# Loading the head's W1 chunks of block 0 in pairs, as 1 KB runs

## The chip, the cores and the metric

One core of one Trainium2 chip runs the whole kernel. The metric is the device time of one execution in microseconds (us). The three sets of experiments ran on chips 5, 14 and 12, so times are compared within a set, and a kernel of one set with one of another only by way of their ratios to the kernel before. A profile shows one execution; its span, from the first instruction to the last, is 1.7 to 1.8 us shorter than that execution's time.

## The reference

```python
y = _layernorm(x)                                             # x: 1 x 2048 x 1024, bf16
h = gelu(einsum("bsd,df->bsf", y, w1) + b1)                   # w1: 1024 x 3584
return einsum("bsf,fd->bsd", h, w2) + b2                      # w2: 3584 x 1024
```

## The kernel before

Both products are done by a Strassen-Winograd scheme: seven half-size products in place of eight, at the price of sums of the inputs (T1 to T4 of the normalized x, S1 to S4 of W1) on the vector engine (DVE). TensorE (PE) is busy nearly all the time. A Python scheduler orders the recorded operations on each engine by their latest useful start, and a packer with a random seed places the buffers.

The argument is about the head, the first 31 us: x is loaded in eight tiles (0 to 7) and normalized; tiles 0 to 3 are transposed on PE, tiles 4 to 7 by DMA (I call these transposes 1 to 4). W1 comes in chunks of 256 columns, each with an upper half of rows (h0) and a lower half (h1), 256 KB each.

```python
def w1_load(b, ch, which, due=None):          # "A1": left columns of W1, "A2": right columns
    i = int(which[1]) - 1
    o = i * FH + ch * 256
    for h in range(2):                        # h0, h1: 4 x 256 columns per partition, runs of 512 B
        bf = W[b, ch, f"{i + 1}{h + 1}"] = M.alloc(KH * 512, f"w1{i}{h}_{b}{ch}")
        pr.due = due if h == 0 else None
        dma("SP", lambda e, h=h, bf=bf: e.dma_start(v3(bf, 0, KH * 512, KH, BF16),
            w1v[:, h * KH:(h + 1) * KH, o:o + 256]), [], [bf.c()], P * KH * 512, None, f"w1{i}{h}_{b}{ch}")
# w1_sums(b, ch): S1 = A21 + A22, S2 = S1 - A11, S3 = A11 - A21, S4 = A12 - S2     (DVE, L799)
# tsum(b, t):     T1 = B12 - B11, T2 = B22 - T1, T3 = B22 - B12, T4 = B21 - T2     (DVE, L763, per tile)
# ... the head, cut:
for ch in range((RH + 1) // 2 - 1):           # chunks 0 to 4: not gated
    w1_load(0, ch, "A1", ...)
# ... waves: first products of rows 0 to 6, one token tile at a time, while the tiles arrive
if t == W_GATE[0]:                            # gated: not before wave 3's first part
    gate[0] = pr.last_pe
    w1_load(0, 5, "A1")                       # chunk 5, h0 and h1
    gate[0] = None
if t == W_GATE[1]: ...                        # the same with w1_load(0, 0, "A2")
# ...
for r in range(RH):                           # RH = 11: 15 products of 4 matmuls
    if r + 1 >= WAVE_ROWS and r + 1 < RH:
        p1(r + 1)                             # first product: needs h0
    p2(r)                                     # second product: needs h1
warm(1, bank=7, full=True)                    # one filler matmul
# then row 0's sixth product, the first that needs T2 (all four tiles) and S2 (chunk 0)
```

## Time and profile before

| | before |
|---|---|
| median of the first three executions | 333.7 us (333.12 to 333.77) |
| the profiled execution | 334.54 us, span 332.8 us |
| PE busy | 326.7 us, 98% of the span |
| first of the 15 products starts (same profile) | 16.06 us |
| long run of PE after the filler starts (same profile) | 30.77 us |

### The profile page before, as it was taken

What the parts mean: (1) busy time and instruction counts of PE and PEld (TensorE: products, weight loads), DVE (VectorE), ACT (ScalarE), POOL (GpSimd) and SP (SyncE); (2) the same over time, 40 slices, a digit from 0 to 9 for tenths busy, and PEclk for the clock granted to TensorE, in tenths of its full rate; (3) what the DMA queues carried; (4) which work ended last, traced back from release to release, by engine and by line L of the source; (5) the groups of instructions that cost most, each with busy time, mean ns of one, the idle gap of its engine ahead of it and who ended that gap; (6) DMA issues with size and microseconds to landing.
All of it is one profiled execution on the core that took longest, in us unless ns stands there. A gap on an engine that the chain in (4) does not pass through costs nothing.

```text
span 332.8 us, 4656 instructions
## 1 busy us (share of the span) xinstructions
PE 326.7 (98%) x1672; PEld 154.8 (47%) x1673; DVE 298.9 (90%) x478; ACT 181.0 (54%) x308; POOL 13.7 (4%) x31
## 2 busy tenths in 40 slices
PE   8998999999999999999999999999999999999996
PEld 5843444444444444444444444444444444444445
DVE  5968999999999975999699998999999959999994
ACT  4795999997677776677776553561211204211411
POOL 2210120111000000000000000000000000000000
PEclk9999999999999999999999999999999999999999
DMA  7997997979999899989969464555699767999867
GB/s 220 326 181 196 282 290 221 295 215 301 307 291 327 281 294 342 310 297 386 336 187 259 147 185 115 163 156 176 176 238 254 221 198 183 273 279 292 192 149 164
DMA packets 121184, 80.73 MB, mean 243 GB/s; under 512 B 35146, under 2 KB 112586, under 8 KB 121162
## 3 DMA queue, kind: packets, MB, share of 16 engines
q1 hardware_dynamic: 118106, 79.32, 84.3%
q10 hardware_dynamic: 3056, 1.11, 1.3%
q8 instruction: 13, 0.21, 0.3%
q14 instruction: 9, 0.07, 0.1%
HBM read 48.70 MB, written 24.38 MB: 220 GB/s over the span
## 4 chain that ended last, share of the span: by engine, by line
PE 90%; DMA 5%; DVE 3%; SPq 1%; issue 0%; POOL 0%
PE ps L934 45%; PE ps L1276 44%; DMA mem<-mem 2%; DMA mem<-in_x_dram 2%; DMA mem<-in_w_dram 1%; DVE st_sb L688 1%; PE ps L1283 1%; DVE mem L763 1%; SPq L787 1%; DVE mem L695 0%; SPq L658 0%; POOL rstd_sb L692 0%; SPq L745 0%; DVE mv_sb L690 0%; PE ps L1156 0%
## 5 line engine op out<-in xcount | busy, mean ns | idle before, releaser
L934 PE MATMUL ps<-mem 128*128 128x512 f16 x756 | 164.1, 379 | 1.4 <-DMA mem<-in_w_dram 1.4
L1276 PE MATMUL ps<-mem 128*128 128x512 f16 x672 | 145.7, 379 | 0.0
L934 PEld LDWEIGHTS ps<-mem 128*128 128x128 f16 (+1 forms) x756 | 73.7, 98 | 90.8 <-ACT mem L843 1.8
L859 ACT COPY mem<-ps 128x512 f32<-128x512 f32 x111 | 64.5, 588 | 76.0 <-PE ps L1276 62.1
L1276 PEld LDWEIGHTS ps<-mem 128*128 128x128 f16 (+1 forms) x672 | 65.8, 98 | 79.3
L843 ACT ACTIVATE mem<-ps,b_sb 128x512 f16<-128x512 f32 x112 | 73.5, 691 | 22.6 <-DVE ps L867 12.9
L867 DVE TENSOR_TENSOR ps<-ps,mem 128x512 f32<-128x512 f32 x84 | 58.0, 695 | 11.7 <-ACT mem L859 8.6
L1091 DVE TENSOR_TENSOR mem<-mem 128x2048 f16<-128x2048 f16 (+1 forms) x56 | 59.3, 1085 | 1.6 <-PE ps L1276 1.6
L799 DVE TENSOR_TENSOR mem<-mem 128x1024 f16<-128x1024 bf16 (+1 forms) x56 | 37.9, 685 | 1.8 <-DMA mem<-in_w_dram 1.2
L1000 DVE TENSOR_TENSOR mem<-mem 128x512 f16<-128x512 f16 (+5 forms) x84 | 37.3, 462 | 0.4
L1103 DVE TENSOR_TENSOR mem<-mem 128x2048 f16<-128x2048 f16 (+1 forms) x32 | 33.6, 1087 | 0.4 <-PE ps L934 0.4
L850 ACT COPY ps<-ps 128x512 f32<-128x512 f32 x31 | 17.7, 570 | 23.4 <-DVE mem L1175 14.8
L1175 DVE TENSOR_TENSOR mem<-ps,mem 128x512 f32<-128x512 f32 x24 | 16.5, 685 | 3.9 <-PE ps L1276 3.7
L688 DVE BATCH_NORM_STATS2 st_sb<-mem 128x6 f32<-128x512 bf16 x24 | 15.4, 674 | 4.0 <-DMA mem<-in_x_dram 4.0
L984 DVE TENSOR_TENSOR mem<-mem 128x2048 f16<-128x2048 bf16 (+1 forms) x16 | 17.3, 1082 | 0.0
L1128 DVE TENSOR_TENSOR mem<-ps,mem 128x512 bf16<-128x512 f32 x22 | 15.0, 688 | 1.3 <-PE ps L1276 1.2
L763 DVE TENSOR_TENSOR mem<-mem 128x512 f16<-128x512 f16 x32 | 12.1, 419 | 2.5 <-DMA mem<-mem 2.3
L692 POOL TENSOR_TENSOR rstd_sb<-mv_sb,nhalf 128x1 f32<-128x1 f32 x12 | 8.4, 699 | 45.6 <-DVE mv_sb L690 44.4
L1262 ACT COPY ps<-b_sb 128x512 f32<-128x512 f32 x6 | 3.5, 588 | 8.2 <-DVE mem L1175 8.0
L695 DVE TENSOR_SCALAR mem<-mem,mv_sb,rstd_sb 128x1024 f16<-128x1024 bf16 (+1 forms) x13 | 6.6, 518 | 1.4 <-POOL rstd_sb L692 1.4
L1351 PE MATMUL ps<-mem 128*128 128x128 f16 x112 | 7.3, 219 | 0.3 <-DMA mem<-in_w_dram 0.3
L1306 PE MATMUL ps<-const-bfloat16-1.0 128*128 128x128 bf16 (+1 forms) x35 | 6.0, 350 | 1.4 <-PEq L1607 0.8
(45 smaller groups left out, 73.3 us busy)
## 6 DMA issues: line engine op xcount, KB each, us to landing
mem<-in_w_dram SPq DMA_DIRECT2D x80, 256.0 KB, 4.9
mem<-w_scr SPq DMA_DIRECT2D x28, 448.0 KB, 3.9
w_scr<-mem SPq DMA_DIRECT2D x21, 512.0 KB, 5.1
w_raw<-mem SPq DMA_DIRECT2D x12, 512.0 KB, 5.6
mem<-w_raw SPq DMA_DIRECT2D x12, 448.0 KB, 4.4
mem<-in_w_dram SPq DMA_DIRECT2D x9, 448.0 KB, 4.1
mem<-in_x_dram SPq DMA_DIRECT2D x15, 256.0 KB, 4.3
out_dram<-mem SPq DMA_DIRECT2D x12, 256.0 KB, 3.9
```

The costliest lines, as they stand in the source:

```text
L688: op("DVE", 0.62, lambda e, i=i, h=h: e.bn_stats(st_sb[:, i, 6 * h:6 * (h + 1)], v16(b, h * D, D, BF16)), r=[b.c(h)], w=[c_st[i][h]], name ...
L799: op("DVE", d_tt(n), lambda e: e.tensor_tensor(out=o[0], in0=a[0], in1=bb[0], op=f), r=[a[1], bb[1]], w=[o[1]], name=f"w1S{k}_{ch}")
L843: op("ACT", A_GELU, lambda e: e.activation(out=dst, in_=banks[bank][:, :], func=ACT.Gelu_apprx_tanh, bias=b1_sb[:, f:f + 1], scale=1.0), r ...
L850: op("ACT", A_CP, lambda e: e.copy(out=banks[dst][:, :], in_=banks[src][:, :]), r=[bank_c[src]], w=[bank_c[dst]], name=name, lat=A_LAT)
L859: op("ACT", A_CP, lambda e: e.copy(out=v16(a, 0, 2048, F32), in_=banks[src][:, :]), r=[bank_c[src]], w=[a.c()], name=name, lat=A_LAT)
L867: op("DVE", D_PS, lambda e: e.tensor_tensor(out=banks[dst][:, :], in0=banks[src][:, :], in1=v16(a, 0, 2048, F32), op=ALU.add), r=[bank_c[s ...
L934: i = e.matmul(banks[bank][:, :], lhsT=lv[:, k, :], rhs=rv[:, k, :], start=(fresh and k == 0), stop=(k == KH - 1), skip_group_check=True)
L984: op("DVE", d_tt(2 * self.n), lambda e: e.tensor_tensor(out=vd, in0=va, in1=vb, op=ALU.subtract), r=self.cells(a) + self.cells(bb), w=self ...
L1000: tt = lambda o, a, c: (lambda e: e.tensor_tensor(out=o, in0=a, in1=c, op=ALU.subtract))
L1091: op("DVE", d_tt((k1 - k0) * 512), lambda e, a=a, bb=bb, o=o: e.tensor_tensor(out=o, in0=a[0], in1=bb[0], op=f), r=a[1] + bb[1], w=[t.c(z) ...
L1103: op("DVE", d_tt((k1 - k0) * 512), lambda e, va=va, vb=vb, vd=vd: e.tensor_tensor(out=vd, in0=va, in1=vb, op=f), r=h_cells(b, a, s, k0, k1 ...
L1276: i = e.matmul(banks[bank][:, :], lhsT=bv[:, k, :], rhs=av3[:, k, :], start=(fresh and k == 0), stop=(k == KQ - 1), skip_group_check=True)
```

## The change

Its intent: fewer, longer loads where the DMA queue of the head is full, and the lower half of chunk 5 earlier. Chunks 0 to 3 keep single h0 loads; h1 of chunks 0 and 1, h1 of 2 and 3, h0 of 4 and 5 and (gated) h1 of 4 and 5 become pairs of 512 KB with 1 KB runs, each in one buffer that lives until both chunks have let it go. The packer's seed changes.

```diff
-SEED = 18
+SEED = 17
+            def w1_block(b, chs, i, h, due=None):
+                n = len(chs)
+                o = i * FH + chs[0] * 256
+                bf = M.alloc(KH * 512 * n, f"w1{i}{h}_{b}{chs[0]}")
+                uses = [n]
+                ...
+                dma("SP", lambda e: e.dma_start(v3(bf, 0, KH * 512 * n, KH, BF16), w1v[:, h * KH:(h + 1) * KH, o:o + 256 * n]),
+                    [], [bf.c()], P * KH * 512 * n, None, f"{'w1' if n == 1 else 'W1'}{i}{h}_{b}{chs[0]}")
 ...
-            for ch in range((RH + 1) // 2 - 1):
-                w1_load(0, ch, "A1", (None, W_DUE[ch]) if ch < len(W_DUE) else None)
+            for ch in range(4):
+                w1_block(0, (ch,), 0, 0, (None, W_DUE[ch]) if ch < len(W_DUE) else None)
+            w1_block(0, (0, 1), 0, 1)
+            w1_block(0, (2, 3), 0, 1)
+            w1_block(0, (4, 5), 0, 0)
 ...
-                    w1_load(0, (RH + 1) // 2 - 1, "A1")
+                    w1_block(0, (4, 5), 0, 1)
```

More of the change, by code (lines that the diff above doesn't have):

```diff
@@ L778, in build, with w1_load, w1_view @@
             W = {}
-            def w1_load(b, ch, which, due=None):
-                i = int(which[1]) - 1
-                o = i * FH + ch * 256
-                for h in range(2):
-                    bf = W[b, ch, f"{i + 1}{h + 1}"] = M.alloc(KH * 512, f"w1{i}{h}_{b}{ch}")
-                    pr.due = due if h == 0 else None
-                    dma("SP", lambda e, h=h, bf=bf: e.dma_start(v3(bf, 0, KH * 512, KH, BF16), w1v[:, h * KH:(h + 1) * KH, o:o + 256]),
-                        [], [bf.c()], P * KH * 512, None, f"w1{i}{h}_{b}{ch}")
-                pr.due = None
+            w1_part = {}
+            def w1_block(b, chs, i, h, due=None):
[3 more added lines that the diff above has]
+                uses = [n]
+                for z, ch in enumerate(chs):
+                    W[b, ch, f"{i + 1}{h + 1}"] = bf
+                    w1_part[b, ch, f"{i + 1}{h + 1}"] = z, n, uses
+                pr.due = due
+                dma("SP", lambda e: e.dma_start(v3(bf, 0, KH * 512 * n, KH, BF16), w1v[:, h * KH:(h + 1) * KH, o:o + 256 * n]),
+                    [], [bf.c()], P * KH * 512 * n, None, f"{'w1' if n == 1 else 'W1'}{i}{h}_{b}{chs[0]}")
+                pr.due = None
+            def w1_load(b, ch, which):
+                for h in range(2):
+                    w1_block(b, (ch,), int(which[1]) - 1, h)
+            def w1_view(b, ch, k, dt):
+                bf = W[b, ch, k]
+                z, n, _ = w1_part.get((b, ch, k), (0, 1, None))
+                return v3(bf, 0, KH * 512 * n, KH, dt)[:, :, z * 256:(z + 1) * 256], bf.c()
             def w1_sums(b, ch):
                 n = KH * 256
-                A = lambda k: (v16(W[b, ch, k], 0, n * 2, BF16), W[b, ch, k].c())
-                S = lambda k: (v16(W[b, ch, k]), W[b, ch, k].c())
+                A = lambda k: w1_view(b, ch, k, BF16)
+                S = lambda k: w1_view(b, ch, k, F16)
                 def mk(k, a, bb, f):
@@ L808, in lhs1 @@
                 k = {1: "11", 2: "12", 4: "22", 3: 4, 5: 1, 6: 2, 7: 3}[q]
-                bf = W[b, ch, k]
-                return v3(bf, 0, KH * 512, KH, BF16 if q in (1, 2, 4) else F16)[:, :, rr:rr + P], bf.c()
+                v, c = w1_view(b, ch, k, BF16 if q in (1, 2, 4) else F16)
+                return v[:, :, rr:rr + P], c
             def w1_drop(b, ch, which):
-                M.free(W.pop((b, ch, which)))
+                bf = W.pop((b, ch, which))
+                uses = w1_part.pop((b, ch, which), (0, 1, [1]))[2]
+                uses[0] -= 1
+                if not uses[0]:
+                    M.free(bf)
             H = {}
@@ L1325, in build @@
             dma("SP", lambda e: e.dma_start(b1r_sb[FT:NBR, :], b2.rearrange("(t p) -> t p", p=P)), [], [c_b2r], D * 2, None, "b2")
-            for ch in range((RH + 1) // 2 - 1):
-                w1_load(0, ch, "A1", (None, W_DUE[ch]) if ch < len(W_DUE) else None)
+            assert (RH + 1) // 2 == 6
+            for ch in range(4):
[3 more added lines that the diff above has]
+            w1_block(0, (4, 5), 0, 0)
             for i in range(4):
```

## The prediction

> **What bounds the kernel now.** I began with the page's busy shares, because they say how much there is to win at all:
>
> ```profile
> PE 326.7 (98%) x1672; PEld 154.8 (47%) x1673; DVE 298.9 (90%) x478; ACT 181.0 (54%) x308; POOL 13.7 (4%) x31
> ```
>
> TensorE (PE) is busy nearly the whole span: only 332.8 - 326.7 = 6.1 us are not matmul time. PE's waits show which part of that waits for something:
>
> ```profile
> PE ps L934 <- DMA mem<-in_w_dram: 1.4, 1, 1.4
> PE ps L1306 <- PEq L1607: 0.8, 1, 0.8
> PE ps L1306 <- DVE st_sb L688: 0.6, 1, 0.6
> PE ps L1351 <- DMA mem<-in_w_dram: 0.3, 1, 0.3
> ```
>
> The middle two belong to the start. The 1.4 and the 0.3 us are waits for W1 loads, which the change touches. The chain that ended last tells where the long one lies (start, length, what):
>
> ```profile
> 25.03 4.53 DMA mem<-in_w_dram
> 29.55 0.14 issue
> 29.69 1.02 PE ps L934 x4
> 30.71 0.05 issue
> 30.77 147.79 PE ps L934 x684
> ```
>
> A W1 load issued at 25.03 us lands at 29.55, and PE goes on at 29.69. From 30.77 the chain is PE alone until 329.77: later than this no earlier load can win anything. The timeline of 0 to 32 us shows the gap and the order of the loads on the SP queue (L787 is a W1 load, L745 a transpose by DMA):
>
> ```profile
> 14.62 4.31 SPq L745 DMA_TRANSPOSE mem<-mem  x2
> 16.06 12.25 PE L934 MATMUL ps<-mem 128*128 128x512 f16 x56
> 18.98 0.58 SPq L787 DMA_DIRECT2D mem<-in_w_dram  x1
> 19.60 4.18 SPq L745 DMA_TRANSPOSE mem<-mem  x2
> 20.05 3.02 DVE L763 TENSOR_TENSOR mem<-mem 128x512 f16<-128x512 f16 x8 [0.68 <-DMA mem<-mem]
> 23.82 2.82 SPq L787 DMA_DIRECT2D mem<-in_w_dram  x5
> 24.71 3.02 DVE L763 TENSOR_TENSOR mem<-mem 128x512 f16<-128x512 f16 x8 [1.64 <-DMA mem<-mem]
> 28.04 3.84 DVE L799 TENSOR_TENSOR mem<-mem 128x1024 f16<-128x1024 bf16 x6 [0.31 <-DMA mem<-in_w_dram]
> 29.69 2.53 PE L934 MATMUL ps<-mem 128*128 128x512 f16 x10 [1.38 <-DMA mem<-in_w_dram]
> ```
>
> By the source, PE does 15 products of 4 matmuls after the waves: the second products ("p2") of rows 0 to 10, which read the lower half of W1's rows (h1), with the first products of rows 7 to 10 between. 56 matmuls are 14 of them; the one that stalls is p2 of row 10, and it reads chunk 5's h1. That load is the third of the five at 23.82, behind all four transposes. Chunk 5's other half (h0), at 18.98, came in good time.
>
> **What the Trainium skill says.** "DMA: Bandwidth & Descriptors", section "Why small descriptors are slow (HBM only)", puts a fixed overhead of about 3 cycles on each packet beside one cycle for 32 bytes. By its arithmetic 512 B take 19 cycles and 1 KB takes 35, so two 512 B runs cost 38: an 8% gain in the DMA engines, an estimate from that page. Its section "Specifications" gives about 358 GB/s as the HBM limit of a core. The trace leaves little room below that: 331 to 338 GB/s moved in 8 to 14 us, where the queue is full with 512 B W1 runs and 2 KB x rows. So I take the longer run itself for a small thing. The same page, "Rules for kernel authors", advises to issue a load early and wait late; the trace agrees: the load that was issued 4.5 us before its landing stalled PE, the one at 18.98 didn't. "Perfetto Trace Analysis", section on the HWDGE instruction, says that the window shown of a DMA instruction is descriptor generation, not data movement. The trace agrees: a transpose's window on SP is 1.4 to 2.83 us, its landing comes 3.1 to 5.4 us after its start.
>
> **The change part by part.**
>
> Removed: in the head 10 ungated loads of 256 KB plus two gated become 4 single ones of 256 KB and three pairs of 512 KB ungated, plus one gated pair. Bytes are the same (12 x 256 KB = 3 MB), ungated bytes too (2.5 MB); 4 instructions on SP fewer, 0.45 to 0.98 us each, but most of that lies in SP's wait for a full queue. The 8% on the 1.5 MB that are ungated and paired, at 335 GB/s (4.5 us), gives 0.3 us at most of an earlier empty queue near 14 to 17 us. There the transposes wait for the norm (L695) and PE for no load, so next to nothing of it reaches the end.
>
> Moved, and this matters: the gated pair (chunks 4 and 5, h1) now carries what stalled. The build's order puts it right after the first two transposes, in the slot of 18.98, not in that of 25.03. There a load of 256 KB took 4.8 us to land. The other half adds 256 KB at 300 GB/s, 0.9 us: landing at 18.98 + 4.8 + 0.9 = 24.7. The first that needs it is p2 of row 8, the 12th product. A matmul takes 12.25/56 = 0.219 us, so it starts at 16.06 + 44 x 0.219 = 25.7. A margin of 1.0 us: the wait of 1.38 us goes, and PE ends the 15 products and the filler matmul at 16.06 + 61 x 0.219 = 29.4 in place of 30.77. That is the gross gain: **1.4 us**. The 0.3 us wait stays: the first four W1 loads and the x loads around them keep their order.
>
> Given back: in the new order the fourth transpose stands behind the third and three loads of the "A2" half of W1 (before: the third and fourth together, then the loads). The next PE work, the sixth product of row 0, needs the T2 sums of all four token tiles and W1's S2 sums. DVE's order in the build is now: T sums of tiles 0 to 2 (12 operations), chunk 0's W1 sums (4), then tile 3's T sums (4). Third transpose issued at about 19.5, landing as before at 24.7 (its tile's sums end at 26.2). A2 loads from 22.4 in steps of 0.6, the first two landing after 3.6 to 4.2 us as at 23.82: about 26.4 and 26.9. Chunk 0's W1 sums then run from 26.4 to 26.4 + 4 x 0.64 = 29.0 (3.84/6 = 0.64 us each). Fourth transpose from 24.2, landing 3.1 to 5.1 us later: 27.3 to 29.3. Tile 3's T1 and T2 take 2 x 0.38 (3.02/8): T2 is ready at 29.0 or 29.3 + 0.76 + some 0.15 for the semaphore, 29.9 to 30.2. So PE waits 0.5 to 0.8 us where it is now ready at 29.4.
>
> Sum: 30.77 less about 30.05 is **0.7 us net**; 333.7 - 0.7 = 333.0.
>
> The seed of the buffer packing changes as well (18 to 17), and one buffer of 512 KB lives as long as the later of its two chunks. That moves all later addresses and so the waits of loads for freed buffers. PE has no wait there now, so this can only cost. I put it at 0 to 0.5 us; against it stands the chance that the fourth transpose lands early, so I leave the centre almost there: 332.9.
>
> **The rivals.** (1) The whole 1.4 us comes: if T2 is ready by 29.4. For it: the scheduler sees these waits and ordered the work so. Against: DVE has 8 operations to do between about 26.4 and then. Time: 332.3. (2) The new wait for the fourth transpose takes all: it is issued 1.8 us later than now, behind three loads on a queue that moves 280 to 300 GB/s at 26 to 30 us. If it lands at 30 or later, PE starts at 31 or after: 333.7 to 334.2. (3) The pair of 512 KB lands after 25.7, as it shares the engines with the third transpose: a stall at p2 of row 8 in place of row 10. 0.5 us of it would still be hidden, since PE then waits for T2 anyway. (4) The longer run speeds the whole head up by 2 us or so: against it speaks that PE's head before 16 us waits for x and the norm, not for W1. (5) A new buffer wait after 40 us: up to 1 us lost.
>
> **Range and chances.** The best case, all waits gone and nothing new, is 332.2; with a run-to-run spread of 0.3 us (333.12 to 333.77 before) 332.0 is the low end. The high end is rival 2 or 5 in full: 334.0. Two per cent are 6.7 us; the head has only 1.7 us of waits for W1, and nothing in the order of PE changes, so both outer chances are about 1%.
>
> **What would show it.** Right, step by step: PE's wait of 1.4 us for a W1 load is gone from the waits; the gated 512 KB load is issued near 19 us; a PE wait of 0.3 to 1 us for DVE (a T sum) appears near 29.5; the long run of first-half products starts at 29.9 to 30.3 and is as long as before, 147.8 us. Wrong: a PE wait for a W1 load near 25.7 (rival 3); a DVE wait for a transpose over 1.5 us near 29 (rival 2); the waves ending clearly before 16.0 us (rival 4); any PE gap after 31 us (rival 5).

## The result, and the profile after

Six executions each: the changed kernel took 333.82 us (median, 333.16 to 334.37), the one before 333.76 (333.12 to 333.95). The ratio is 1.0003, with a 95% interval of 0.999 to 1.0017. The time is inside the predicted range, and "within 2%" was right; of the 0.8 us that the centre promised, nothing came.

The profiled execution tells another story at first sight. These are all of PE's waits in the changed kernel (who waited, for whom: us in total, times, longest):

```profile
PE ps L1325 <- PEq L1630: 0.8, 1, 0.8
PE ps L1325 <- DVE st_sb L688: 0.6, 1, 0.6
PE ps L1374 <- DMA mem<-in_w_dram: 0.4, 1, 0.4
```

The wait of 1.4 us for W1 is gone. PE's timeline has the start of the long run:

```profile
29.41 2.97 PE L953 MATMUL ps<-mem 128*128 128x512 f16 x13
```

The long run starts 1.36 us earlier than before (30.77), the span is 331.4 in place of 332.8 us, and no new wait stands at 29.4. But this execution took 333.16 us, the fastest of the six, while the profiled one of before, 334.54, was slower than all six of its timed ones in that set. The two profiles are from opposite ends of two spreads that lie on each other. (334.54 is not rare either: in the later sets 8 of 33 executions of the kernel before took 334.5 us or more.) The timeline shows the new order on the SP queue and on DVE (L792 is now a W1 load, L814 a W1 sum):

```profile
14.83 3.00 SPq L745 DMA_TRANSPOSE mem<-mem  x2
...
16.24 13.11 PE L953 MATMUL ps<-mem 128*128 128x512 f16 x60
...
17.87 0.58 SPq L792 DMA_DIRECT2D mem<-in_w_dram  x1
...
18.50 1.27 SPq L745 DMA_TRANSPOSE mem<-mem  x1
...
19.81 2.38 SPq L792 DMA_DIRECT2D mem<-in_w_dram  x3
...
22.23 3.30 SPq L745 DMA_TRANSPOSE mem<-mem  x1
...
23.49 1.56 DVE L763 TENSOR_TENSOR mem<-mem 128x512 f16<-128x512 f16 x4 [1.10 <-DMA mem<-mem]
...
25.68 2.85 DVE L814 TENSOR_TENSOR mem<-mem 128x1024 f16<-128x1024 bf16 x4 [0.64 <-DMA mem<-in_w_dram]
...
28.45 1.55 DVE L763 TENSOR_TENSOR mem<-mem 128x512 f16<-128x512 f16 x4
```

To be seen: the gated load at 17.87 us, the fourth transpose now behind three A2 loads, and on DVE four W1 sums before the T sums of tile 3 (28.45). T2 of that tile is the second of the last four, ready about 29.3.

### The profile page after: what moved, and what is told of

Same layout as the page of the kernel before. It is cut to its first block, busy times and chain, and to the rows that moved or that the text cites. A ratio compares the mean times of both kernels' runs of the same rounds, so it can differ in the third digit from the quotient of the medians.

```text
span 331.4 us, 4655 instructions
## 1 busy us (share of the span) xinstructions
PE 326.6 (99%) x1673; PEld 154.8 (47%) x1673; DVE 299.6 (90%) x478; ACT 181.0 (55%) x308; POOL 14.3 (4%) x31
## 4 chain that ended last, share of the span: by engine, by line
PE 96%; DMA 2%; SPq 1%; DVE 0%; issue 0%
PE ps L953 49%; PE ps L1295 44%; DMA mem<-in_w_dram 2%; PE ps L1374 2%; PE ps L1302 1%; SPq L658 0%; SPq L792 0%; PE ps L720 0%; PE ps L1175 0%; DVE mem L1264 0%; SPq L655 0%; PE ps L1325 0%; PE ps L1386 0%
## 5 line engine op out<-in xcount | busy, mean ns | idle before, releaser
L814 DVE TENSOR_TENSOR mem<-mem 128x1024 f16<-128x1024 bf16 (+1 forms) x56 | 37.9, 684 | 3.1 <-DMA mem<-in_w_dram 2.8
```

The lines of the kernel that those rows point to most:

```text
L814: op("DVE", d_tt(n), lambda e: e.tensor_tensor(out=o[0], in0=a[0], in1=bb[0], op=f), r=[a[1], bb[1]], w=[o[1]], name=f"w1S{k}_{ch}")
```

## The experiments

**The theories.** Theory A: the start of the long run is the latest of three times: (w) the start of the 15 products plus 13.17 us (29.41 - 16.24 in the first profile of the changed kernel); (l) the landing of chunk 5's h1, plus its product and the filler; (s) the T2 and S2 sums on DVE. The executions differ in all three, and the first two profiles are not the usual case. Theory B, the rival: the head does win its 1.4 us always, and the changed kernel loses it again later, by buffers or order. Rival C: the W1 wait of 1.4 us is usual before, and the changed kernel turns it into a usual T2 wait of equal size. Rival 4 of the prediction, that the run length matters by itself, is also open.

### Both kernels profiled again: b_again and a_again

No edit. First the kernel before, then the changed one:

> The kernel before, unchanged, for a second profile. Its first profile had a span of 332.8 us, 0.8 over what its median time implies (333.76 less the 1.75 us by which time exceeds span in the runs after). Theory A (the head's wait varies from run to run, and the first profile caught a long one): span about 332.0, the W1 wait before row 10's second product clearly under 1.4 us, 0 to 0.9, so that the long run of PE starts at 29.4 to 30.3. Theory B (the wait is always there and the changed kernel loses its gain later): the wait is again 1.3 to 1.5 us and the start 30.7 to 30.9, with fewer than 302.0 us from there to the end. Ratio to before 1.000.

> The changed kernel, unchanged. Its profiled run was the fastest of six (333.16 against a median of 333.82). Theory A (my T2 term): a typical run has a PE wait of 0.3 to 1 us near 29.4 for a T sum, so the start of the long run is 29.9 to 30.3. Theory B: no wait near 29.4, start at 29.5 to 29.7 as in the first profile, and 302.3 to 302.7 us from there to the end in place of 301.8. Ratio to before 1.000 by both.

Measured: b_again 333.65 us (6 runs) and a_again 334.02 (5), before 334.02 (11 in the same rounds); ratios 0.9992 and 1.0005. The waits of PE in the kernel before, second profile, all of them:

```profile
PE ps L1306 <- PEq L1607: 0.8, 1, 0.8
PE ps L1306 <- DVE st_sb L688: 0.7, 1, 0.7
```

The W1 wait isn't there at all. The timeline of the same profile:

```profile
7.10 1.06 PE L720 MATMUL ps<-ident,mem 128*128 128x128 f16 x8
...
16.80 13.11 PE L934 MATMUL ps<-mem 128*128 128x512 f16 x60
...
19.22 2.67 SPq L745 DMA_TRANSPOSE mem<-mem  x2
...
21.94 3.51 SPq L787 DMA_DIRECT2D mem<-in_w_dram  x5
...
29.96 2.32 PE L934 MATMUL ps<-mem 128*128 128x512 f16 x10
```

Two things moved: the five loads were issued from 21.94 and not from 23.82 us, and the products began at 16.80 and not at 16.06. The first is why there is no W1 wait: the third of the five, issued at 23.85, landed at 28.0 and not at 29.55, and even with products from 16.06 PE would have come to it at 28.1 (it came at 28.88). The second sets the long run, at 29.96 us (case w). The products were late because PE was slow at the beginning: the first eight transposes took 1.06 us, in the first profile 0.72. The Trainium skill, "TensorE: Matmul & The Clock Gate", section "Part 1: The HAM clock gate", says that PE begins at half clock and that its release varies from run to run, as a free-running activity window decides it. The trace agrees in size, counted from the start of one group of matmuls to that of the next: 0.86/8 = 0.107 us for a transpose from 7.10 to 7.96, against 0.45/8 = 0.056 from 9.46 to 9.91. So late a start happened in two of the fourteen profiles (the other is a_512b).

The changed kernel's second profile, its waits for the head's data and its timeline:

```profile
PE ps L953 <- DVE mem L763: 0.7, 1, 0.7
...
PE ps L1374 <- DMA mem<-in_w_dram: 0.2, 1, 0.2
```
```profile
15.95 13.11 PE L953 MATMUL ps<-mem 128*128 128x512 f16 x60
...
25.03 1.55 DVE L763 TENSOR_TENSOR mem<-mem 128x512 f16<-128x512 f16 x4 [2.50 <-DMA mem<-mem]
...
26.50 2.61 DVE L814 TENSOR_TENSOR mem<-mem 128x1024 f16<-128x1024 bf16 x4
...
29.04 1.55 DVE L763 TENSOR_TENSOR mem<-mem 128x512 f16<-128x512 f16 x4
...
29.97 2.33 PE L953 MATMUL ps<-mem 128*128 128x512 f16 x10 [0.69 <-DVE mem L763]
```

PE is ready at 29.3 and waits 0.69 us for a T sum. DVE idled 2.50 us for transpose 3, whose data landed at 25.03 (23.49 in the first profile); from there it has no gap: T sums of tile 2, four W1 sums (S3, S1, S2 of chunk 0 and S3 of chunk 1), then tile 3. The predicted T2 wait is real, and the first profile had missed it by a lucky landing. Theory B falls: the long run and all after it is as long in both kernels (time less start of the long run: 303.8 us in all four profiles). So an execution's time tells its start: the median of the kernel before, 333.98 us over all 39 executions, stands for 30.2, and that of the changed kernel, 333.87 over 11, for 30.1.

### The move alone: b_move and b_swap

The first try gave both halves of chunk 5 a due time, so that the scheduler should place h1 behind h0:

```diff
-                    pr.due = due if h == 0 else None
+                    pr.due = due if h == 0 and due else (pr.last_pe, 4.0) if (b, ch, which) == (0, 5, "A1") else None
```

> The kernel before with one thing moved: chunk 5's lower half is issued right behind its upper half, after the second transpose, not behind the fourth. No pairs, seed 18, transposes 3 and 4 still together. If the moved load is the whole of the gain: the PE wait for W1 at row 10 is gone, PE is ready at 29.4; the A2 loads come one slot (0.6 us) earlier than before. Theory A: ratio 0.998 to 1.000 (gain up to 0.6 us, as the typical wait is short). Theory B: the start of the long run falls by 1.3 us, ratio 0.996 to 0.997.

Measured: 336.35 us, ratio 1.0074 (1.006 to 1.0088). The head was better, with the long run at 29.66 us, but the scheduler had reordered hundreds of later instructions, and a wait of 1.3 us for DVE opened near the end (the chain runs over DVE from 317.6 to 320.4). So its time tells nothing of the move. The second try changes the recorded order itself, after the scheduler (after_of is printed with the next experiment), and the two programs then differ in this one place:

```diff
         pr = best
+        after_of("w101_05", "w100_05")    # chunk 5: h1's start directly behind h0's
```

> The kernel before with one instruction moved on the SP queue and nothing else: chunk 5's lower half directly behind its upper half, ahead of transposes 3 and 4. Its four A2 loads then come one issue (0.6 us) earlier. Theory A (the start of the long run is the latest of three: the end of the waves + 13.3 us; the W1 load + 1.1 us; the sums on DVE, and the first profile caught a rare case of the second): no W1 wait, start set by the waves or by S2, 29.3 to 29.9 where waves begin near 16.0; ratio 0.998 to 1.000. Rival C (the W1 wait of 1.4 us is the usual case and the changed kernel lost it again to its own T2 wait): ratio 0.996 to 0.997.

Measured: 334.31 us, before 334.23; ratio 1.0002 (0.9978 to 1.0026). No gain, though no W1 wait is left. Its timeline:

```profile
15.96 13.11 PE L934 MATMUL ps<-mem 128*128 128x512 f16 x60
...
28.68 3.82 DVE L799 TENSOR_TENSOR mem<-mem 128x1024 f16<-128x1024 bf16 x6 [0.58 <-DMA mem<-in_w_dram]
...
30.24 2.97 PE L934 MATMUL ps<-mem 128*128 128x512 f16 x13 [1.16 <-DVE mem L799]
```

All 60 matmuls run through, and PE then waits 1.16 us for the S2 sum, whose A2 load had landed at 28.68. So taking the wait for W1 away uncovers one for the sums. Its size of 1.16 us can't be carried over to the kernel before: there, in the first profile, the six sums began at 28.04, which by the same distance (30.24 - 28.68 = 1.56 us) would have let PE go on at 29.6, 0.4 us after it was ready (16.06 + 13.17 = 29.2). In b_move, with the same order in the head, they began at 28.19 and PE waited 0.44 us. Whether the later A2 load of b_swap is chance or comes of the edit, which issued transposes 3 and 4 at 20.38 and not at 19.60, stays open. Rival C's ratio (0.996 to 0.997) lies outside the interval: moving this load alone does not win 1.4 us. That doesn't tell how usual the W1 wait is; a_again, the medians above and b_fill below do, as far as it is known.

### What T2 waits for: a_s3late, a_s3late2

Two of the four W1 additions that stand before tile 3's T sums aren't needed by the next product: S3 of chunks 0 and 1.

```diff
         pr = best
+        def after_of(name, other, n=0):       # the first task of that name, moved behind the other
+            t, o = (sorted((t for t in pr.tasks if t.name == z), key=lambda t: t.start)[0] for z in (name, other))
+            t.start = o.start + 1e-4
+        after_of("w1S3_0", "T2_03")
+        after_of("w1S3_1", "T4_03")
```

> The changed kernel with two DVE additions for W1 (S3 of chunks 0 and 1, 0.65 us each) moved behind tile 3's T2 and T4 sums; nothing else moves. If the first product after the second products waits for DVE's queue (theory A): T2 is ready up to 1.3 us earlier, the PE wait for a T sum (0.7 us in the second profile) is under 0.3, ratio 0.997 to 0.999 of before. If it waits for the landing of the fourth transpose instead: DVE idles before tile 3's sums, the wait stays at 0.5 to 1.0, ratio 1.000.

Measured: 332.98 us (332.75 to 333.31) against 334.23 before; ratio 0.9961 (0.9938 to 0.9984). The profile:

```profile
15.72 17.52 PE L953 MATMUL ps<-mem 128*128 128x512 f16 x79
...
24.75 1.55 DVE L763 TENSOR_TENSOR mem<-mem 128x512 f16<-128x512 f16 x4 [2.67 <-DMA mem<-mem]
...
26.34 1.42 DVE L814 TENSOR_TENSOR mem<-mem 128x1024 f16<-128x1024 bf16 x2
...
28.02 0.89 DVE L763 TENSOR_TENSOR mem<-mem 128x512 f16<-128x512 f16 x2 [0.27 <-DMA mem<-mem]
```

Tile 3's sums start at 28.02, 1.0 us earlier than in a_again, of which 0.3 us comes from transpose 3's landing (24.75 against 25.03), and PE passes from the products into the long run with no wait (79 matmuls in one row; start of the long run 28.97 us). DVE now waits 0.27 us for transpose 4: that landing is next in line, and it was hidden while DVE had other work (in a_again it came at 28.3, and the sums only at 29.04). A second set:

> The changed kernel with the two S3 additions behind tile 3's T sums, a second time, for a second profile and a second interval. If the first result (0.9961) stands: start of PE's long run 28.8 to 29.4, no PE wait for DVE above 0.3 us, ratio 0.995 to 0.998. If it was luck of the waves' start: 0.998 to 1.000.

333.22 us against 333.98, ratio 0.998 (0.9963 to 0.9997), long run at 29.16, PE's wait for a T sum 0.28 us. In both sets it is faster than the kernel before, by 0.4 and 0.2% (1.25 and 0.76 us by the medians), which the changed kernel isn't. It was not run in the same rounds as the changed kernel, but each against before; a_seed18 below, the changed kernel with the other seed, did share the second set's rounds and took 334.3 us, 1.1 us more. This is the version to keep.

### The run length: a_512, a_512b and a_s3_512

Order, buffers and seed of the changed kernel, but each pair's load is issued as two DMAs into the halves of its buffer, with 512 B runs:

```diff
-                dma("SP", lambda e: e.dma_start(v3(bf, 0, KH * 512 * n, KH, BF16), w1v[:, h * KH:(h + 1) * KH, o:o + 256 * n]),
+                one = lambda e, z: e.dma_start(v3(bf, z * KH * 512, KH * 512, KH, BF16),
+                                               w1v[:, h * KH:(h + 1) * KH, o + 256 * z:o + 256 * (z + 1)])
+                t = dma("SP", lambda e: [one(e, z) for z in range(n)] if n > 1 else one(e, 0),
 ...
+                t.nd = n                # waits count 16 for each of the n DMAs
```

> The changed kernel with the same order, buffers and seed, but each pair loaded by two DMAs of 256 KB with 512 B runs. If the longer run matters (rival 4): the waves end later and the landing of chunks 4 and 5's lower half is over 1 us later, ratio to before 1.002 or more. If only the order matters (mine): the gated halves land within 0.5 us of the changed kernel's, no new PE wait, ratio within 0.001 of a_again.

> The changed kernel with 512 B runs again, for a second profile of the wait of 1.9 us for a T sum that the first showed. If the runs' length matters: wait over 1.0 us again, transpose 3 landing at 25.5 or later, ratio 1.001 to 1.003. If the first was a slow case: wait 0.3 to 1.0, as with 1 KB runs, ratio 1.000.

The third is the same edit on a_s3late:

> The same with every pair loaded as two DMAs with 512 B runs, same order and buffers. With DVE's detour gone, the landing of transposes 3 and 4 sets T2. If the 1 KB runs matter there: those landings come 0.5 to 1.0 us later, a PE wait for a T sum of 0.5 to 1.2 us, ratio 0.002 to 0.003 above a_s3late2. If they don't: equal within 0.001.

| kernel | ratio to before (95%) | transpose 3's sums start | long run starts |
|---|---|---|---|
| a_again, 1 KB | 1.0005 (0.9991 to 1.0019) | 25.03 | 29.97 |
| a_512 | 1.0014 (1.0001 to 1.0027) | 25.93 | 30.87 |
| a_512b | 1.0006 (0.9991 to 1.0021) | 25.33 | 30.27 |
| a_s3late2, 1 KB | 0.998 (0.9963 to 0.9997) | 24.96 | 29.16 |
| a_s3_512 | 0.9996 (0.9981 to 1.0012) | 25.78 | 30.19 |

In the clean pair, the last two rows, which shared their rounds, the split pairs cost 0.8 us by the medians (333.22 and 334.03) and 1.0 us by the start of the long run; the other pair points the same way, within its noise. The edit changes two things at once, though: the runs are shorter, and each pair is two DMAs. The second DMA of the gated pair takes SP 0.6 us more to issue (1.17 us for both in a_s3_512, 0.58 for one in a_s3late2), and transpose 3 follows it, issued at 20.03 and not at 18.48. Two DMAs of 1 KB runs, cut by partitions, would tell the two apart; that was not run. Nor is transpose 3's landing always later: a_seed18, with 1 KB runs, has 25.43, a_512b 25.33. The stretch from 9 to 14 us, where the queue is full of x and W1, shows that the rate differs as well. Its columns: the stretch and its length, busy time of PE, PE's weight loads, DVE, ACT and POOL, the granted clock, the DMA engines' busy share, GB/s. First the kernel before, then a_again, then a_512:

```profile
9.00:14.00 5.00, 4.71 (x85) 4.54 (x83) 4.49 (x10) 2.74 (x7) 1.82 (x3) 1.00 1.11 338
```
```profile
9.00:14.00 5.00, 4.75 (x86) 4.58 (x84) 4.49 (x11) 2.86 (x8) 1.85 (x3) 1.00 1.07 363
```
```profile
9.00:14.00 5.00, 4.92 (x89) 4.75 (x87) 4.76 (x12) 2.94 (x7) 1.71 (x3) 1.00 1.12 338
```

All eight profiles with 512 B runs gave 338 or 339 GB/s there, the six with 1 KB runs 356 to 367: a gain of 5 to 9%. Here too the longer runs come in DMAs of twice the size. The Trainium skill's arithmetic in "DMA: Bandwidth & Descriptors", section "Why small descriptors are slow (HBM only)", 38 cycles against 35, an estimate of 8%, fits it in size.

### Filling the wait: a_fill and b_fill

Row 11's first product needs only loaded data, so it was moved ahead of row 0's sixth product:

```diff
-            flat = []
+            flat = [((0, RH), 1)]
 ...
-                flat += [(g, 1)] + ([(prev, 7)] if k else []) + [(g, 5), (g, 2), (prev, 4), (g, 6), (prev, 3)]
+                flat += ([(g, 1)] if k else []) + ([(prev, 7)] if k else []) + [(g, 5), (g, 2), (prev, 4), (g, 6), (prev, 3)]
```

> The changed kernel with one product of 4 matmuls (0.86 us), the first of row 11, moved to stand before the first product that needs T and S sums. It needs only what has landed, so it fills a wait for DVE if there is one. Theory A: the PE wait for the T sum near 29.4 falls by 0.86 us or vanishes; the gain is the typical wait, 0.5 to 0.9 us, ratio 0.997 to 0.999, unless the reordered rest opens a wait later (to be read past 31 us). Theory B (no such wait in a typical run): ratio 1.000.

> The kernel before with the same product moved to the same place. Its wait, where it has one, is for W1 ahead of this place, and DVE's sums are done when PE arrives: nothing to fill, ratio 0.999 to 1.001 by theory A. If a sum were the limit here too, 0.997 to 0.999.

Measured: 338.56 us, ratio 1.0114 (1.0082 to 1.0146), and 335.22 us, ratio 1.0026 (1.0003 to 1.0049). The times tell nothing of the head: as in b_move, the scheduler moved the rest, and a_fill's PE waits 1.9 us for a load of a stored W2 sum, b_fill's 0.6 us for DVE in the second half. As timings these two are failures of the method.

But b_fill's profile is a third sample of the kernel before up to the last of the 15 products, as nothing ahead of it was moved. PE stops at the same place as in the first profile, after 56 matmuls:

```profile
29.04 4.26 PE L934 MATMUL ps<-mem 128*128 128x512 f16 x18 [0.88 <-ACT mem L843]
```

The profile puts the wait down to ScalarE, but ScalarE isn't the cause: in b_swap the same L843 instruction ended at 29.08, and PE did the same product from 28.05 on without a stop. The load of chunk 5's h1, issued at 24.69, landed 4.2 us later, at 28.9, and PE went on 0.14 us after that, as in the first profile (29.55, 29.69). So this is the W1 wait again: 1.4, 0 and 0.9 us in three profiles.

### The seed: a_seed18

```diff
-SEED = 17
+SEED = 18
```

> The changed kernel with the buffer packing seed of the kernel before (18). The order of the head is the same; only addresses and the order after about 35 us differ. If the packing matters (rival 5 of the prediction): a PE wait after 31 us, ratio 1.001 or more. If not: start of the long run as in a_again, 302 us to the end, ratio 1.000.

334.3 us, before 333.98; ratio 1.0004 (0.9987 to 1.0021). No PE wait after 31 us, and PE's wait for the T sum before it was 1.0 us:

```profile
25.43 1.55 DVE L763 TENSOR_TENSOR mem<-mem 128x512 f16<-128x512 f16 x4 [2.75 <-DMA mem<-mem]
...
30.38 2.98 PE L953 MATMUL ps<-mem 128*128 128x512 f16 x13 [1.01 <-DVE mem L763]
```

So no effect of the packing is seen, within the interval's 0.2%, and as the head's order is that of the changed kernel, this is a third sample of it: T2 waits of 0, 0.7 and 1.0 us.

## Why the prediction was right or wrong

The range and the class held, the range in part by luck: 333.82 lies near its upper end, in the stretch that I had given to rival 2 (the fourth transpose takes all), which is not what happened. Point by point:

- **The gross gain of 1.4 us** is the term that failed. The wait was in the profiled execution, and the step "30.77 less about 30.05 is 0.7 us net; 333.7 - 0.7 = 333.0" took the head of an execution of 334.54 us off the median of others. Counted from the same execution it gives 334.54 - 0.7 = 333.8, which is what was measured (333.82). The start that I forecast for the changed kernel, about 30.05, was right: its median less the 303.8 us that follow the start is 30.0. What failed is the 30.77 that it was held against: the median of the kernel before, 333.76, stands for 30.0 too. The W1 wait was 1.4 us in the one profile that I had, and 0 and 0.9 us in the next two.
- **The second wait behind it**: I took the W1 wait for the whole loss. Before, the S2 sum stands behind the W1 load: 0.4 us behind PE's readiness in the first profile, 1.16 us in b_swap, which took the load's wait away alone and had a ratio of 1.0002.
- **The gated pair lands in time**: right. No profile of the changed kernel has a PE wait for it. It was issued at 17.9, 1 us earlier than I put it, as the first two transposes ahead of it took SP 3.0 us and not 4.3.
- **Given back, a T2 wait of 0.5 to 0.8 us**: right in size (0, 0.7, 1.0 in three profiles). The cause was partly another: I set the later fourth transpose beside DVE's queue as equals; a_s3late shows that DVE's queue binds, from transpose 3's landing on, and that the fourth transpose comes next: DVE waits 0.27 us for it once two additions are out of the way.
- **"Next to nothing" from 1 KB runs**: probably wrong. The rate grew as estimated, past the 358 GB/s that I had taken for a ceiling (up to 367), but I looked only at what PE waits for, and not at the transposes behind the loads. Their landing goes into T2. a_s3_512 puts the pairs, longer runs and fewer DMAs together, at 0.8 us of the time once DVE's detour is gone; before that most of it is covered. The share of the run length alone is not shown.
- **The waves' start as a constant**: wrong. 15.6 to 16.8 us over the profiles, the late ones from PE's slow start.
- **The seed** (rival 5): no PE wait after 31 us in the changed kernel's profiles with either seed; the 0 to 0.5 us I set aside weren't needed.
- **Slips that change little**: 12.25/56 counts the tail of the last matmul. From start to start a matmul takes 13.17/61 = 0.216 us, so PE was ready at 29.2 and not at 29.4. The 0.98 us of an SP instruction is two of them. The queue moved 273 to 300 GB/s at 26 to 30 us, not 280 to 300. Of the four W1 sums ahead of tile 3 three are chunk 0's.

So where did the gain go? The W1 wait was removed, but the start that it set was usually earlier than in the profile (30.0 to 30.2 by the medians, not 30.77), and DVE's sums stood behind it; the new order moved tile 3's sums behind four W1 additions, and the changed kernel spends 0 to 1 us there.

What stays open: how often the W1 wait, the S2 wait and late products each set the start before (three profiles, W1 waits of 1.4, 0.9 and 0), why transpose 3 landed at 23.5 in the first profile of the changed kernel (23.57 in a_fill) and at 25.0 to 25.4 in others, and what the longer runs are worth without the smaller number of DMAs.

## What to carry to other kernels

Compare the profiled execution's time with the median before you subtract a wait that it shows: here the two differed by more than the whole gain. Where a wait ends, list all things that the next instruction needs and when each is ready, as the second latest is what you will wait for next. A name in a profile's wait is a guess to be checked against another run in which the same thing didn't stop the engine. And test a move by editing the finished order: a scheduler that is given a new hint changes far more than the hint.

## What the Trainium skill lacked or had wrong

- "DMA: Bandwidth & Descriptors", "Specifications", gives some 358 GB/s as the HBM limit of a core, without a condition; only its section "Bandwidth" says that this is a core's share when both cores of a pair stream. One core ran here and moved up to 367 GB/s over 5 us (a_s3late, 9 to 14 us), so the figure isn't contradicted, but the row by itself misled the prediction. The page's per-packet arithmetic was right in size (8% estimated, 5 to 9% measured).
- The same page has a bandwidth for DMA transposes, but I found nothing on how long one takes to land among queued loads: 5.0 us from its start in one execution (18.50 to 23.49) and 6.5 in another of the same kernel (18.57 to 25.03).
- "TensorE: Matmul & The Clock Gate" has the run-to-run variation of the slow start, and warns that clock events in a trace can be unreliable. The granted clock of the profile reads 1.00 from 7 to 8.5 us in b_again, where eight transposes took 1.06 us, and in the first profile, where they took 0.72.
